# An S4 convolution with a gated FFN, forward and backward: the SSM kernel factored over 128 centred inner and 16 outer positions instead of 64 and 32

## The chip, the core and the metric

The program runs on one core of one Trainium2 chip. Its engines work side by side and each takes its instructions in order from its own queue: TensorE (matmuls, with weight loads that overlap them), VectorE, ScalarE, GpSimd, and SyncE, which here only issues DMAs. The metric is the time on the device, in microseconds (us). The kernel before took 2039.39 us, the median of five runs that lay between 2024.03 and 2045.57.

## The reference, cut to what matters

One layer with a sequence of L = 2048 positions, D = 576 channels, N = 128 states per channel and F = 4608 hidden units, in bf16. The program returns the layer's output and the gradients by twelve inputs.

```python
xn = _layernorm(x)
dt = exp(log_dt)                                   # one per channel
P  = exp((dt * (A_re + 1j*A_im))[:, :, None] * l)  # D x N x L, l = 0 .. L-1
K  = einsum("dn,dnl,dn->dl", C, P, dt * B).real    # the convolution kernel, D x L
s  = causal_convolution(xn, K) + xn * Dskip        # by FFT in the reference
g  = silu((silu(xn @ w1) * (xn @ w3)) @ w2)
out = x + s * g
# and the vector-Jacobian product of out with grad_out, by x, A_re, A_im,
# B_re, B_im, C_re, C_im, log_dt, Dskip, w1, w3, w2
```

For the gradients by A, B, C and log_dt four sums over l are needed for every channel and state: the kernel's gradient gK, and l times gK, each against the real and the imaginary part of P.

## The kernel before, in words

**Order of work.** All code is written for a planner that compiles it: `at(us)` (L83) gives the instructions that follow a due time, and the planner sorts each engine's queue by these times and by what is ready. Pools of SBUF and PSUM buffers (`tile_pool`, `bufs=n`) add waits: a tile is not written before the last reader of the buffer's former tile is done, and a pool's space is not used before the pool that held it is closed. Once built, each queue is fixed and in order.

**The factored exponential.** P at position l = AV-index and BV-index, l = BV*a + b, is the product of an outer and an inner exponential. With BV = 64 and AV = 32 (L36) the tables hold, for 16 channels (a "chunk", 36 of them), 16 x 64 inner columns called q and 16 x 32 outer ones called p or pz, 128 states deep. `build_selectors` (L336) makes two matrices of small numbers on VectorE and GpSimd: SELR and SEL. A matmul of the channels' rates with SELR gives the arguments of the real exponentials, one with SEL gives those of the phases.

**Prologue (0 to 135 us).** Layernorm, the DFT matrices dC, dSf, dSi, the selectors; then `early_exps` (L376) makes the tables E of all chunks, two chunks to a tile: matmuls into PSUM tiles of 1024 columns, Exp on ScalarE (L392), a store to E_dram. `early_spectra` (L395) makes the input's spectra beside it. The FFN's PSUM pools take the space of these two.

**Forward FFN (135 to 532 us).** `ffn_hidden` (L688): nine blocks of 512 hidden units, products of xn with w1 and w3 (L719 to L721), Silu, stores of h, of the gate and of the up product. Between its matmuls `ssm_kernel` (L418) runs, one chunk every 8.7 us by the due times. `kgen_chunk` (L455) makes the phases in PSUM tiles `et_ps` of a pool with one buffer, sine and cosine (`trig`, L326), the products q and pz with E, and v, the outer factor times B and C; q goes to Q_dram, pz to PZ_dram. `kgen_sum` (L490) contracts q with v over the 128 states, for each channel in two halves of 64 rows (L500), and copies the kernel K to the SBUF tensor KT.

**Forward tail (540 to 790 us).** `forward_tail`: h times w2 (`po`, L784), the convolution through DFTs of 1024 points in blocks of 512 (`spectra_quarter`, `conv_quarter`), a quarter of the channels at a time, and the output.

**Backward (790 to 2029 us).** `backward` (L1066) lays three things beside each other:
- 18 FFN groups of 256 hidden units (`phase6_group`, L1158, until 1627 us): the gradient of h (`ph`, L1173, copied by ScalarE at L1176), of w2 (L1201) and of w1 and w3 (L1220). The transposed gradients of gate and up go to GG_dram and GU_dram.
- Kernel gradients, 860 to 1310 us: `ssm_bwd_conv` and `conv_bwd_quarter` (L867). Inverse DFTs (`idft_tile`, matmul at L582) give gK for 128 positions at a time. ScalarE writes it from PSUM to `gk_st`, four times for each tile: two halves of the channels, plain (L927) and times l (L928). Stores bring it to gK_dram.
- Parameter sums from 1316 us on: `param_quarter` (L951). For each chunk SyncE loads the gradients into one of three buffers `gz`, whose other halves were set to zero once, transposes Q_dram to qT (L1124, called for qT), and loads pz. TensorE multiplies qT with gz (L971), VectorE multiplies with pz (L978) and sums (L980) into S_all. Their chunks have due times TC = 15 us apart.

What is left of the parameter sums runs beside the last stage, `phase6_inputs` (L1235), 1639 to 1988 us: 16 tiles of 128 positions, each with transposed loads ggc and guc (SyncE), 144 matmuls with the weights (`px`, L1263), and the layernorm's gradient (`ln_bwd_tile`, VectorE, ending at L1292 with the output tile). `phase5_final` (L983) turns S_all into the parameter gradients: four transposes on TensorE per 128 channels, then small VectorE steps.

Of the kernel before, what the change touches and what calls it, by code (L numbers as in the profile page):

```python
# [11 lines left out]
ALU = mybir.AluOpType  # L12
# [4 lines left out]
P = 128  # L17
# [5 lines left out]
class Cfg:  # L23
# [12 lines left out]
    AV: int = 32  # L36
    BV: int = 64

    @staticmethod
    def make(L, D, N, F, LS=None):  # L40
# [13 lines left out]
        assert L % 64 == 0  # L54
        c.AV = L // 64
        c.BV = 64
        assert c.AV % 2 == 0 and c.AV <= 64
# [3 lines left out]
class K:  # L61
# [24 lines left out]
    def setup_consts(self):  # L86
# [18 lines left out]
        nc.vector.tensor_copy(out=self.pcol[:], in_=icol[:])  # L105
        W = 512
# [219 lines left out]
    def trig(self, sb, m, nbits, n_el, tagp):  # L326
        nc = self.nc
        S = sb.tile([P, n_el], BF16, name="S_" + tagp)
        nc.scalar.activation(out=S[:], in_=m[:], func=ACT.Sin, scale=6.283184 / 2 ** nbits)
        A = m[:].bitcast(FP32)  # L330
        nc.scalar.activation(out=A, in_=m[:], func=ACT.Abs, scale=2.0 ** -nbits)
        C = sb.tile([P, n_el], BF16, name="C_" + tagp)
        nc.scalar.activation(out=C[:], in_=A, func=ACT.Sin, scale=-6.283184, bias=self.halfpi_col[:])
        return S, C

    def build_selectors(self, st, selp):  # L336
        nc, cfg = self.nc, self.cfg
        AV, BV, DC = cfg.AV, cfg.BV, 16
        QW, PW = DC * BV, DC * AV
        self.SEL = selp.tile([P, QW + PW], BF16, name="SEL")  # L340
        SELR = st.tile([P, QW + PW], BF16, name="SELR")
        ii = st.tile([P, QW + PW], I32, name="ii")
        i2 = st.tile([P, QW + PW], I32, name="i2")
        val = i2[:].bitcast(FP32)
        nc.gpsimd.iota(ii[:, 0:QW], pattern=[[1, DC], [0, BV]], base=0, channel_multiplier=0)
        nc.gpsimd.iota(ii[:, QW:], pattern=[[1, 2], [2, DC // 2], [0, AV]], base=0, channel_multiplier=0)
        nc.gpsimd.iota(i2[:, 0:QW], pattern=[[0, DC], [1, BV]], base=0, channel_multiplier=0)
        nc.gpsimd.iota(i2[:, QW:], pattern=[[0, DC], [1, 2], [2, AV // 2]], base=0, channel_multiplier=0)
        dl = ii[:].bitcast(FP32)
        nc.vector.tensor_copy(out=dl, in_=ii[:])  # L350
        nc.vector.tensor_copy(out=val, in_=i2[:])
        pi_ = st.tile([P, 1], I32, name="pi_")
        nc.gpsimd.iota(pi_[:], pattern=[[1, 1]], base=0, channel_multiplier=1)
        pmi = st.tile([P, 1], I32, name="pmi")
# [5 lines left out]
        rc = st.tile([P, 1], FP32, name="rc")  # L360
        nc.vector.tensor_scalar(out=rq[:], in0=self.pcol[:], scalar1=48.0, scalar2=None, op0=ALU.is_lt)
# [3 lines left out]
        nc.vector.tensor_scalar(out=rc[:], in0=self.pcol[:], scalar1=112.0, scalar2=96.0, op0=ALU.is_equal,  # L365
                                op1=ALU.mult)
        nc.vector.scalar_tensor_tensor(out=val, in0=dl, scalar=pm[:, 0:1], in1=val, op0=ALU.is_equal,
                                       op1=ALU.mult)
        nc.vector.tensor_copy(out=SELR[:, 0:QW], in_=val[:, 0:QW])
        nc.vector.tensor_scalar(out=SELR[:, QW:], in0=val[:, QW:], scalar1=float(BV), scalar2=None, op0=ALU.mult)  # L370
        for (sl, rr) in ((slice(0, QW), rq), (slice(QW, QW + PW), rp)):
            nc.gpsimd.tensor_scalar(out=self.SEL[:, sl], in0=val[:, sl], scalar1=rr[:, 0:1], scalar2=rc[:, 0:1],
                                    op0=ALU.mult, op1=ALU.add)
        return SELR

    def early_exps(self, SELR, LR_, ep, ps):  # L376
# [6 lines left out]
        for c2 in range(0, NCH, 2):  # L383
            E = ep.tile([P, 2, TW], BF16, name="E_k")
            Ef = E[:].rearrange("p c t -> p (c t)")
            for o in range(0, 2 * TW, 1024):
                pe = ps.tile([P, 1024], FP32, name="e_ps")
                for k in range(2):
                    ch, o1 = divmod(o + 512 * k, TW)
                    nc.tensor.matmul(pe[:, 512 * k:512 * k + 512], lhsT=LR_[:, c2 + ch, :], rhs=SELR[:, o1:o1 + 512],  # L390
                                     start=True, stop=True)
# [997 lines left out]
```

## Time and profile before

| | |
|---|---|
| median of five runs | 2039.39 us |
| the profiled execution, its time on the device | 2030.45 us |
| its span in the trace | 2028.7 us |
| mean granted clock of TensorE | 0.957 of full speed |
| busy: TensorE, its weight loads | 1749.6 us (86%), 1289.4 us (64%) |
| busy: VectorE, ScalarE, GpSimd | 1428.9 us (70%), 991.8 us (49%), 256.0 us (13%) |
| DMA traffic | 416.04 MB, mean 205 GB/s |
| FFN matmuls L719, 1088 of them | 273.4 us, 380 ns each |
| pr_q products L978, 288 of them on VectorE | 186.7 us, 682 ns each |
| S_all sums L980, 144 of them on VectorE | 174.1 us, 1212 ns each |
| last-stage matmuls L1263, 2304 of them | 482.5 us, 289 ns each |

All rows but the first two are of one execution, recorded by the profiler. Busy times of engines overlap, so they do not add up to the span; matmuls are pipelined, so what one costs is read from the starts of a row of them rather than from its duration. Lines such as L978 are lines of the kernel's code above. "Idle before, releaser" in a row is the time that the engine stood before these instructions and what let it go on. A share of busy time is a mean over stages with different limits; the stretches and the waits tell them apart.

### The profile page before, as it was taken

To read this page: it belongs to the slowest core of one execution; us is meant where nothing else is said; L and a number is where in the kernel's file an instruction comes from. 1 tells how busy PE (TensorE), PEld (TensorE's weight loads), DVE (VectorE), ACT (ScalarE), POOL (GpSimd) and SP (SyncE) were. 2 spreads that over 40 slices of the span, in tenths; PEclk is the share of its full clock that TensorE was granted. 3 is DMA by queue.
4 is the path that set the end of the run, shared out by engine and by line. 5 is a ranking of instruction groups with operands and counts; after the bars stand their busy time and mean duration, and the time that the engine had idled before them with its cause. 6 is when DMAs were issued, how large, how long until landed. Compare 5 with 4: busy or idle time off the path is not lost. (4 is left out here: it accounts for less than half of the span.)

```text
span 2028.7 us, 41789 instructions
## 1 busy us (share of the span) xinstructions
PE 1749.6 (86%) x17103; PEld 1289.4 (64%) x17174; DVE 1428.9 (70%) x2772; ACT 991.8 (49%) x1668; POOL 256.0 (13%) x324
## 2 busy tenths in 40 slices
PE   2789999999699996889889899889898938899991
PEld 1444444444478875778778777778776826777781
DVE  7548888888387732586884868767888555677777
ACT  2778888888545543775656746544454300000000
POOL 4003333333331102000000000100000000000000
PEclk9899999999899998899999999999999969999996
DMA  3588888897956558565473655799789599999971
GB/s 85 193 296 308 301 296 304 280 324 269 284 159 168 155 129 236 152 178 166 148 196 115 186 158 156 197 261 253 191 224 192 145 210 222 209 225 229 234 151 20
DMA packets 615088, 416.04 MB, mean 205 GB/s; under 512 B 403185, under 2 KB 560753, under 8 KB 610289
## 3 DMA queue, kind: packets, MB, share of 16 engines
q1 hardware_dynamic: 553264, 282.87, 55.5%
q0 software_dynamic: 23056, 105.00, 15.0%
q10 hardware_dynamic: 38576, 25.50, 4.6%
q8 instruction: 134, 2.20, 0.4%
q14 instruction: 58, 0.47, 0.1%
HBM read 133.01 MB, written 188.01 MB: 158 GB/s over the span
## 5 line engine op out<-in xcount | busy, mean ns | idle before, releaser
L719 PE MATMUL pgu<-wmB_w,xnT 128*128 128x512 bf16 x1088 | 273.4, 380 | 6.4 <-issue 3.2
L978 DVE TENSOR_TENSOR pr_q<-et_ps,pz 128x512 f32<-128x512 f32 x288 | 186.7, 682 | 111.1 <-PE et_ps L971 80.9
L1263 PE MATMUL px<-wTB_w,guc 128*128 128x288 bf16 x1152 | 240.5, 289 | 26.4 <-DMA guc<-GU_dram 14.2
L1263 PE MATMUL px<-wTB_w,ggc 128*128 128x288 bf16 x1152 | 242.0, 289 | 14.3 <-DMA wTB_w<-in_B_w_dram 9.4
L1220 PEld LDWEIGHTS <-xn_bf 128*128 128x128 bf16 x2304 | 226.2, 98 | 42.3 <-issue 13.9
L1173 PE MATMUL ph<-w2T,goT 128*128 128x256 bf16 x1440 | 191.7, 282 | 28.6 <-ACT gh L1176 25.9
L719 PEld LDWEIGHTS <-xnT 128*128 128x128 bf16 x1152 | 103.1, 98 | 124.0 <-issue 18.9
L980 DVE TENSOR_REDUCE S_all<-pr_q 128x16 f32<-128x1024 f32 x144 | 174.1, 1212 | 0.4
L1280 ACT ACTIVATE t<-gx 128x576 f32<-128x576 f32 x16 | 10.9, 684 | 332.9 <-DVE gx L1266 332.9
L1173 PEld LDWEIGHTS <-goT 128*128 128x128 bf16 x1440 | 141.5, 101 | 50.6 <-issue 26.7
L1201 PE MATMUL pgw<-go_o,h_n 128*128 128x288 bf16 x1152 | 156.8, 290 | 7.8 <-DVE h_n L1155 7.8
L1222 ACT CAST gw<-pgw 128x256 bf16<-128x256 f32 x144 | 54.0, 378 | 202.7 <-PE pgw L1220 195.4
L784 PE MATMUL po<-w2g,hc 128*128 128x288 bf16 x1152 | 148.6, 286 | 1.7 <-DMA hc<-H_dram 1.7
L1263 PEld LDWEIGHTS <-guc 128*128 128x128 bf16 x1152 | 113.0, 99 | 57.1 <-DMA guc<-GU_dram 15.9
L1263 PEld LDWEIGHTS <-ggc 128*128 128x128 bf16 x1152 | 112.4, 99 | 42.5 <-issue 9.5
L1220 PE MATMUL pgw<-gu_n,xn_bf 128*128 128x256 bf16 x1152 | 132.3, 272 | 5.4 <-ACT gw L1205 2.0
L1201 PEld LDWEIGHTS <-h_n 128*128 128x128 bf16 x1152 | 112.4, 99 | 37.6 <-DVE h_n L1155 8.3
L1220 PE MATMUL pgw<-gg_n,xn_bf 128*128 128x256 bf16 x1152 | 131.7, 276 | 4.4 <-ACT gw L1222 4.4
L784 PEld LDWEIGHTS <-hc 128*128 128x128 bf16 x1152 | 111.3, 98 | 29.2 <-DMA hc<-H_dram 2.2
L722 ACT ACTIVATE s_t<-pgu 128x512 bf16<-128x512 f32 x144 | 87.3, 609 | 53.7 <-PE pgu L721 53.4
L1176 ACT CAST gh<-ph 128x512 bf16<-128x512 f32 x144 | 83.7, 617 | 51.1 <-PE ph L1173 28.9
L1179 DVE TENSOR_TENSOR gu_n<-gh,gu_n 128x1024 bf16<-128x1024 bf16 x72 | 49.5, 687 | 77.6 <-ACT gh L1176 77.5
(301 smaller groups left out, 3635.3 us busy)
## 6 DMA issues: line engine op xcount, KB each, us to landing
GI_dram<-gu_t POOLq DMA_DIRECT2D x72, 512.0 KB, 5.6
H_dram<-h_t SPq DMA_DIRECT2D x72, 256.0 KB, 5.1
Q_dram<-q_k SPq DMA_DIRECT2D x36, 512.0 KB, 4.7
gg_n<-GI_dram POOLq DMA_DIRECT2D x18, 1024.0 KB, 6.1
h_n<-GI_dram POOLq DMA_DIRECT2D x18, 1024.0 KB, 8.8
GU_dram<-gu_n SPq DMA_DIRECT2D x36, 512.0 KB, 4.6
GG_dram<-gg_n SPq DMA_DIRECT2D x36, 512.0 KB, 6.7
E_dram<-E_k SPq DMA_DIRECT2D x18, 768.0 KB, 3.7
```

The lines of the kernel that those rows point to most:

```text
L719: nc.tensor.matmul(pgu[:, j], lhsT=xnT[:, c, ts], rhs=wm[w][:, c, :], start=(c == 0), stop=False)
L722: nc.scalar.activation(out=s_t[:, :, q, :], in_=pgu[:, 0].rearrange("p (g f) -> p g f", g=ng), func=ACT.Silu)
L784: nc.tensor.matmul(pos[k][:, pi_, 0:pw], lhsT=hcs[k][:, fi, :], rhs=w2[fi][:, po:po + pw], start=(fi == 0), stop=(fi == FT - 1))
L978: nc.vector.tensor_tensor(out=pr[:, r], in0=T[r][:], in1=pz[:, s + r, h * 8:h * 8 + 8, :][:, :, None, :] .to_broadcast([P, 8, 2, AV]), op= ...
L980: nc.vector.tensor_reduce(out=S_all[:, 2 * s:2 * s + 2, d0:d0 + 8].rearrange("p k d -> p d k"), in_=pr[:].rearrange("p r d k a -> p d k r ...
L1173: nc.tensor.matmul(ph[j][:, k, :].rearrange("p (a f) -> p a f", f=P), lhsT=lw, rhs=rh, start=(n == 0), stop=(n == nfull))
L1176: nc.scalar.copy(out=gh[:, j], in_=ph[j][:])
L1179: nc.vector.tensor_tensor(out=t_[:, sl], in0=gh[:].rearrange("p j t f -> p (j t) f"), in1=t_[:, sl], op=ALU.mult)
L1201: nc.tensor.matmul(pgw[pi_][:, 0:pw], lhsT=hn[:, tt, fl * P:(fl + 1) * P], rhs=go_o[:, tt, po:po + pw], start=(tt == 0), stop=(tt == LT - 1))
L1220: nc.tensor.matmul(pw_[:, 0:FG], lhsT=self.xn_bf[:, tt, c * P:(c + 1) * P], rhs=nat[:, tt, :], start=(tt == 0), stop=(tt == LT - 1))
L1222: nc.scalar.copy(out=gw[:, c, :], in_=pw_[:, 0:FG])
L1263: nc.tensor.matmul(px[pi_][:, 0:pw], lhsT=act[:, fi, :], rhs=wT[part][ai][:, f, po:po + pw], start=(fi == 0 and ai == 0), stop=(fi == FT - ...
```

## The change

The inner positions become 128 (BV) and the outer ones 16 (AV). Inner positions are counted from the middle, 63.5, and the upper half is held in reverse order. So the sine of the upper half is that of the lower with its sign turned, the cosine is the same, and phases are made for 64 of the 128 inner positions. E has 16 x (128 + 16) columns a chunk, the phases 16 x (64 + 16).

Because the rows of K now come with the upper half reversed, `flip_quarter` turns them with matmuls by a permutation, in place, once for each quarter of the channels. In the backward pass the inverse DFT uses reversed copies `imats` of its matrices, made on GpSimd, so that gK comes in the same order.

`kgen_sum` uses 128 columns of q as weights and no halves. In `conv_bwd_quarter` two positions' tiles share one PSUM tile; ScalarE writes the plain half of `gk_st`, VectorE the half that is multiplied by l; one store for a quarter replaces two. `param_quarter` takes 128 rows of gK without zeros, three chunks to a load; the qT tile has twice the columns (32 blocks of 128), its pool two buffers instead of three; products and sums are half as many. In `backward`'s call TC goes from 15 to 12 us. The selectors are made as products of small factors. The pool `kg_m` has two buffers instead of three.

```diff
-    AV: int = 32
-    BV: int = 64
+    AV: int = 16
+    BV: int = 128
...
+        nc.gpsimd.tensor_copy(out=self.flip_bf[:, 0:64], in_=self.ident_bf[:, 0:64])
+        nc.gpsimd.tensor_copy(out=self.flip_bf[:, 64:P], in_=self.ident_bf[:, 64:P][:, ::-1])
...
+        nc.vector.tensor_scalar(out=S[:, 0:n_q], in0=S[:, n_q:2 * n_q], scalar1=-1.0, scalar2=None, op0=ALU.mult)
...
-        nc.vector.scalar_tensor_tensor(out=val, in0=dl, scalar=pm[:, 0:1], in1=val, op0=ALU.is_equal,
-                                       op1=ALU.mult)
...
-        for (sl, rr) in ((slice(0, QW), rq), (slice(QW, QW + PW), rp)):
-            nc.gpsimd.tensor_scalar(out=self.SEL[:, sl], in0=val[:, sl], scalar1=rr[:, 0:1], scalar2=rc[:, 0:1],
-                                    op0=ALU.mult, op1=ALU.add)
...
+            eng.tensor_tensor(out=dst.rearrange("p (d b) -> p d b", b=w), in0=v[:, None, :].to_broadcast([P, DC, w]),
+                              in1=M[:, mi, :, None].to_broadcast([P, DC, w]), op=ALU.mult)
...
-                for k in range(2):
-                    ch, o1 = divmod(o + 512 * k, TW)
-                    nc.tensor.matmul(pe[:, 512 * k:512 * k + 512], lhsT=LR_[:, c2 + ch, :], rhs=SELR[:, o1:o1 + 512],
+                w = min(1024, 2 * TW - o)
+                cuts = sorted({o, o + w} | {b for b in (TW, o + 512) if o < b < o + w})
+                for a, b in zip(cuts, cuts[1:]):
+                    ch, o1 = divmod(a, TW)
+                    nc.tensor.matmul(pe[:, a - o:b - o], lhsT=LR_[:, c2 + ch, :], rhs=SELR[:, o1:o1 + b - a],
                                      start=True, stop=True)
-                nc.scalar.activation(out=Ef[:, o:o + 1024], in_=pe[:], func=ACT.Exp)
+                nc.scalar.activation(out=Ef[:, o:o + w], in_=pe[:, 0:w], func=ACT.Exp)
...
+                    if (ch - 2) % 9 == 8:
+                        self.flip_quarter((ch - 2) // 9, ps, T0 + TK * (ch + 1), TK)
...
+    def flip_quarter(self, g, ps, T, TK):
+        nc, LT = self.nc, self.cfg.LT
+        W = self.cfg.D // 4
+        for n, t in enumerate(range(0, LT, 3)):
+            self.at(T + TK * n / 6)
+            w = min(3, LT - t)
+            pt = ps.tile([P, 512], FP32, name="et_ps")
+            pv = pt[:, 0:w * W].rearrange("p (t d) -> p t d", t=w)
+            kt = self.KT[:, t:t + w, g * W:(g + 1) * W]
+            nc.tensor.matmul(pv, lhsT=self.flip_bf[:], rhs=kt, start=True, stop=True)
+            nc.scalar.copy(out=kt, in_=pv)
...
-            for hf in range(2):
-                for k in range(2):
-                    nc.tensor.matmul(kps[64 * hf:64 * hf + 64, dl, :], lhsT=q[:, dl, k, :],
-                                     rhs=v[:, k, e, hf * AH:(hf + 1) * AH], start=(k == 0), stop=(k == 1))
+            for k in range(2):
+                nc.tensor.matmul(kps[:, dl, :], lhsT=q[:, dl, k, :], rhs=v[:, k, e, :], start=(k == 0), stop=(k == 1))
...
+            for i, mat in enumerate((self.dC, self.dSi)):
+                im = kp.tile([P, cfg.KT, cfg.LS], BF16, name=f"imat{i}")
+                vi, vo = (t_[:].rearrange("p k (n s j) -> p (k n) s j", s=2, j=64) for t_ in (mat, im))
+                nc.gpsimd.tensor_copy(out=vo[:, :, 0], in_=vi[:, :, 0])
+                nc.gpsimd.tensor_copy(out=vo[:, :, 1], in_=vi[:, :, 1, ::-1])
+                self.imats.append(im)
...
-                for h in range(2):
-                    pv = pt[:, h * W // 2:(h + 1) * W // 2].rearrange("p (c d) -> p c d", d=8)
-                    nc.scalar.activation(out=st[:, :, 0, :, h, t], in_=pv, func=ACT.Copy, scale=1.0 / 512)
-                    nc.scalar.activation(out=st[:, :, 1, :, h, t], in_=pv, func=ACT.Copy, scale=self.lcol[:, t:t + 1])
...
+                for j in range(2):
+                    self.idft_tile(pt[:, j * W:(j + 1) * W], ZZ, oc + j, mats=self.imats)
+                pv = pt[:, 0:2 * W].rearrange("p (t d) -> p d t", t=2)
+                nc.scalar.activation(out=st[:, 0, :, t:t + 2], in_=pv, func=ACT.Copy, scale=1.0 / 512)
+                nc.vector.tensor_tensor(out=st[:, 1, :, t:t + 2], in0=pv,
+                                        in1=self.lcol[:, None, t:t + 2].to_broadcast([P, W, 2]), op=ALU.mult)
...
-            gK = gz[ch % 3]
-            for k in range(2):
-                nc.sync.dma_start(out=gK[64 * k:64 * k + 64, 1 - k].rearrange("p k f d t -> p (k f d t)"),
-                                  in_=self.gK_dram[g, :, cc].rearrange("p k f d -> p (k f d)"))
-            qT = tqp.tile([P, 16, N], BF16, name="qT")
-            self.nat_transpose(qT[:], self.Q_dram[ch])
+            if cc % GC == 0:
+                gk = gkp.tile([P, 2, 2, 8 * GC, LT], BF16, name="gk_l")
+                nc.sync.dma_start(out=gk[:].rearrange("p k h d t -> p (k h) (d t)"),
+                                  in_=self.gK_dram[g, :, :, :, 8 * cc:8 * (cc + GC), :].rearrange("p k h d t -> p (k h) (d t)"))
+            qT = tqp.tile([P, 16, 2, N], BF16, name="qT")
+            self.nat_transpose(qT[:].rearrange("p d k n -> p (d k) n"), self.Q_dram[ch])
...
-                        nc.tensor.matmul(T[r][:, dd].rearrange("p k (f t) -> p (k f) t", f=2), lhsT=qT[:, dl, :],
-                                         rhs=gK[:, r, :, :, dl, :].rearrange("p k f t -> p (k f) t"),
-                                         start=True, stop=True)
+                        nc.tensor.matmul(T[:, r, :, dd * AV:(dd + 1) * AV], lhsT=qT[:, 2 * dd + h, 1 - r, :],
+                                         rhs=gk[:, :, h, 8 * (cc % GC) + dd, :], start=True, stop=True)
...
-                    pr = qp.tile([P, 2, 8, 2, AV], FP32, name="pr_q")
-                    for r in range(2):
-                        nc.vector.tensor_tensor(out=pr[:, r], in0=T[r][:], in1=pz[:, s + r, h * 8:h * 8 + 8, :][:, :, None, :]
-                                                .to_broadcast([P, 8, 2, AV]), op=ALU.mult)
-                    nc.vector.tensor_reduce(out=S_all[:, 2 * s:2 * s + 2, d0:d0 + 8].rearrange("p k d -> p d k"),
-                                            in_=pr[:].rearrange("p r d k a -> p d k r a"), op=ALU.add, axis=AX.XY)
+                    nc.vector.tensor_tensor(out=pr[:, s].rearrange("p k r x -> p r k x"), in0=T[:],
+                                            in1=pz[:, s:s + 2, h * 8:h * 8 + 8, :].rearrange("p r d a -> p r (d a)")[
+                                                :, :, None, :].to_broadcast([P, 2, 2, 8 * AV]), op=ALU.mult)
+                nc.vector.tensor_reduce(out=S_all[:, :, d0:d0 + 8],
+                                        in_=pr[:].rearrange("p s k r (d a) -> p (s k) d r a", a=AV), op=ALU.add,
+                                        axis=AX.XY)
...
-        k.backward(560, 36, 90, 15, 18, gctx, mats)
+        k.backward(560, 36, 90, 12, 18, gctx, mats)
```

## The prediction

> **What bounds the kernel now.** I read the busy time by stretches first, then what TensorE waited for in each stage, then the order in time at the places that the change touches, and last the chain that ended the run.
>
> The stretches (columns: stretch, its length, then busy time and instructions of TensorE, of its weight loads, VectorE, ScalarE, GpSimd, then granted clock, DMA share and GB/s):
>
> ```profile
> 50.00:100.00 50.00, 37.90 (x239) 24.31 (x242) 26.51 (x43) 38.22 (x36) 0.99 (x2) 0.86 0.55 184
> 200.00:250.00 50.00, 48.74 (x472) 21.91 (x481) 42.26 (x81) 42.42 (x50) 16.73 (x16) 1.00 0.88 307
> 1000.00:1100.00 100.00, 90.80 (x920) 79.01 (x920) 58.15 (x124) 57.23 (x127) 4.29 (x8) 0.97 0.57 165
> 1400.00:1500.00 100.00, 88.94 (x934) 75.19 (x933) 82.64 (x118) 49.44 (x82) 4.83 (x9) 1.00 0.82 220
> 1700.00:1800.00 100.00, 90.94 (x867) 72.16 (x865) 65.25 (x102) 3.88 (x10) 0.00 (x0) 0.98 1.13 213
> 1900.00:2029.00 129.00, 87.80 (x787) 70.16 (x784) 90.74 (x325) 6.81 (x15) 0.00 (x0) 0.86 0.61 117
> ```
>
> TensorE is nearly full in the FFN stage (200 to 250) and 89 to 91% busy in the backward stages, so VectorE time is worth something only where TensorE waits for it. What TensorE waited for from 860 to 1310 us (kernel gradients) and, second fence, from 1310 to 1627 (parameter sums beside the FFN groups), in us, times, longest:
>
> ```profile
> PE et_ps L582 <- ACT gk_st L928: 16.5, 21, 2.1
> PE ph L1173 <- ACT gh L1176: 7.9, 6, 1.9
> ```
> ```profile
> PE ph L1173 <- ACT gh L1176: 18.1, 7, 7.7
> PE et_ps L971 <- DVE pr_q L978: 3.1, 2, 1.8
> ```
>
> SyncE's queue in the last stage has no gap: a tile's two transposes, then a chunk of the parameter sums, until 1927 us.
>
> ```profile
> 1849.61 2.88 SPq L1124 DMA_TRANSPOSE qT<-Q_dram  x1
> 1852.59 0.53 SPq L965 DMA_DIRECT2D pz<-PZ_dram  x1
> 1853.22 7.28 SPq L1124 DMA_TRANSPOSE ggc<-GG_dram  x1
> 1860.59 6.48 SPq L1124 DMA_TRANSPOSE guc<-GU_dram  x1
> ```
>
> The chain that ended last is VectorE's from 1967 us: the final parameter gradients stand between the last tile's TensorE work (ended 1988.1) and its output.
>
> ```profile
> 1953.86 10.59 DMA guc<-GU_dram
> 2013.43 0.82 DVE o L1292
> ```
>
> **The change, stage by stage.** The profiled execution took 2030.45 us (span 2028.7), 9 us below the median of the five, 2039.39. I sum against the first and carry the difference to the median.
>
> Prologue. A chunk's exponential table grows from 1536 to 2304 columns. Rows that cost it (ScalarE and TensorE in order of time):
>
> ```profile
> 129.35 5.60 ACT L392 ACTIVATE E_k<-e_ps 128x1024 bf16<-128x1024 f32 x6 [0.83 <-DMA E_dram<-E_k]
> ```
> ```profile
> 505.25 1.19 PE L500 MATMUL kps<-v_k,q_k 128*64 128x16 bf16 x64
> 506.37 1.90 PE L719 MATMUL pgu<-wmB_w,xnT 128*128 128x512 bf16 x7
> ```
>
> Six take 5.60 us: 0.93 each. A pair of chunks was 3 of them, 2.8 us; it becomes 4 and a half-sized one, 4.25 us. In the changed order 70 of the 180 table matmuls (7 pairs) follow the last spectrum matmul. The FFN can't start before them, since its PSUM is theirs. The tail was 122.6 to 134.2 us, 11.6; it becomes 7 x 4.25 plus about 0.5 a pair of waiting for the larger store (0.83 stood there), 33 us: +21. The 11 pairs that run beside the spectra add about 1. The selectors lose five wide VectorE passes (4.8 us) and 3.3 us of index generation on GpSimd, and gain two products on each; the products of B and C behind them on GpSimd, and so the layernorm behind those on ScalarE, come earlier: -3 (-5 to 0). Sum +19 (12 to 27).
>
> FFN stage. 2304 kernel-sum matmuls become 1152 with weights of 128 columns instead of 64. The 64 above start 1.12 us before the next instruction: 17.5 ns each, 40 us in all. For 128-column weights the nearest row is L971, where 24 took from 1590.44 to 1591.15, 29.6 ns: 33 us, -7. The Trainium skill speaks against any gain here ("TensorE: Matmul & The Clock Gate", LDWEIGHTS): a load costs its columns over 1.2, so half as many loads of twice the columns cost the same, and 128 columns would take 107 ns, 123 us in all, +83. Both rows above are far quicker than that, so I take the row, with 0 as the upper end. The phase matmuls shrink from 1536 to 1280 columns: 36 x 0.5 x 0.215 = -4. The flip adds 24 matmuls of 432 columns, +4, each evicted by ScalarE in about 0.54 us (between L1205's 0.41 for 288 and L1176's 0.62 for 512), through the single PSUM buffer that the phases share. In the changed order they stand 2 or 3 FFN matmuls (0.43 to 0.65 us) apart; what is queued behind a waiting flip on TensorE is the FFN itself. 24 x 0.25 = +6 (0 to 15). ScalarE loses a sixth of its three sine passes (-0.76 us a chunk) and gains 0.36 of flips; VectorE's products double for q and halve for the rest, by 0.69 and 0.42 us a row about even. Both fit beside TensorE. Sum -1 (-13 to +20; the upper end is the third rival's).
>
> Kernel gradients. 256 ScalarE evictions of 72 elements become 32 on ScalarE and 32 on VectorE of 288. The old ones show 0.80 us but start 0.32 apart, so they occupy 82 us, 1.28 a tile. They write single 2-byte elements 64 bytes apart: 4.4 ns each. The new ones write pairs 32 bytes apart. The Trainium skill ("SBUF — State Buffer", Door 1, the cachelines note) has two hits on a 16-byte line running at full rate: then 288 elements cost 0.41 us as in L1205. By the old row, 144 lines at 4.4 ns are 0.63 us, 288 elements 1.27. I take 0.7 on both engines; no row shows VectorE writing so, 0.45 (L1266) to 1.3. ScalarE is then no limit, and the 24 us of the first fence of waits mostly go; VectorE gains 22 us (14 to 42) in a chain that TensorE waits for too. -18 (-27 to +8). GpSimd's four half-reversed copies of the matrices hide, it is 4% busy; the later loads wait for nothing of them.
>
> Parameter sums. A chunk's VectorE work goes from 8 x 0.68 + 4 x 1.21 = 10.3 us to half, 5.15: 186 us in all. Only the waits in the second fence of waits can come back, and 3 of TensorE's 34 us of matmuls by halved columns. Against that the qT transpose doubles to 32 column blocks of 128; the nearest row is ggc with 36 (5.4 to 7.9 us on the queue, median landing 10.0; guc 8.3): 6.2 us and 8.5 to land, instead of 3.35 and 6.3. And its buffers fall from three to two. In the changed order, three chunks to an FFN group, every third chunk's matmuls stand about 5.3 us behind the last use of the buffer that its transpose needs. TensorE waits there 3.2 us, six times: +19. Queued behind that transpose on SyncE are pz, the kernel gradients and the next group's stores and w2T, a group early; VectorE's products for pz wait too. Relief of 10 of the 21 us of waits, and 3 of matmuls: sum +6 (-10 to +30).
>
> Last stage. The first tile's two transposes come one longer qT later: +1. Chunks now end with tile 8 instead of 14. Eight tiles took 1690.5 to 1853.9 us, 163. They now carry 11 chunks at 6.9 us of SyncE (6.2, pz 0.53, a third of gk), 9.5 a tile, beside 10.6 to 12.7 for ggc and guc: about 21.3 a tile, 170. The last seven took 134; free of chunks they are 144 x 0.1226 us and 0.15, 17.8 each, 125. Sum -3 to -4; I take -4 (-12 to +20). The final gradients run beside tiles 9 to 12 instead of after the last. From its last matmul the last tile needs its own five VectorE steps (4.5 us) and its store (about 5) and the closing 1.7: 11 instead of 40.6, -30 (-34 to -25).
>
> 19 - 1 - 18 + 6 + 1 - 4 - 30 = -27: 2003 on the profiled basis, 2012 against the median.
>
> **Rivals.** (a) Slower: the doubled transposes become the bound. For it: SyncE's queue is gapless, DMA share is 1.13 there, two buffers. Against: it has gaps before 1627 us. Each third chunk then costs 6 us more behind stores and pz, +36 instead of +6, and eight tiles 24 us each, +25 instead of -4: +32, 2071. It decides from 0.8 us of TensorE wait a chunk above my sum (27 over 33 chunks). (b) VectorE is what holds the groups: with 83% busy and a relief of 5 us a chunk, 7.5 groups shrink from 40 to 36.5 us, -26 instead of +6, and the gradients give all 27: -68, 1971. Against: the waits name VectorE for 3 us only. (c) The gain goes in the forward pass: q's store doubles, the net is 0.5 MB more a chunk, 307 GB/s at a share of 0.88 becomes about 345, which is share 1.0 at that ratio. Stores then hold back h_t and gu_t, and TensorE: +20 instead of -1, -6, 2033.
>
> **How the numbers follow.** My sum 0.45, within 1997 to 2027 of its own; (a) 0.2, (b) 0.2, (c) 0.15. A measurement of this kernel can tell about 1%, 20 us, from no change. Below 2019 lie (b) and 0.7 of my case: 0.52; above 2060 (a): 0.21; between them 0.27. The range 1971 to 2062 leaves out half of (b) and of (a).
>
> **What would show it.** The first FFN matmul near 154 us instead of 135; the FFN stage still about 395 us long; no wait for gk_st; waits of et_ps for the transposed q between 1310 and 1630; after tile 8 tiles of 17.8 us; about 11 us behind the last matmul. It is wrong if SyncE's transposes of q take over 8 us, if the new evictions take over 1.3, or if flips stop TensorE for over a microsecond each.

## The result: no faster, with large parts moved both ways

Over 43 runs the changed kernel took 2046.98 us (median, 2035.31 to 2074.09); the kernel before took 2045.41 in the 80 runs that there are of it by now. The ratio is 1.0018, 95% interval 1.0005 to 1.0032. Forecast were 2012 us against 2039, a ratio of 0.987. The profiled execution has a span of 2042.7 us, against 2028.7 before, whose execution lies 15 us below the median of its kernel; so the stages below add up to 14 us more where the medians differ by 2.

| stage, by the starts of TensorE's matmuls | before | after | difference | predicted |
|---|---|---|---|---|
| to the first FFN matmul | 135.0 | 162.4 | +27.4 | +19 |
| FFN, to the first product with w2 | 412.3 | 397.2 | -15.1 | -1 |
| forward tail, to the first group's L1201 (after: L1245) | 270.1 | 269.1 | -1.0 | 0 |
| kernel gradients, to the eleventh group | 494.5 | 466.4 | -28.1 | -18 |
| parameter sums, to the first tile | 327.3 | 363.9 | +36.6 | +6 and +1 |
| first eight tiles | 196.0 | 206.7 | +10.7 | +7 |
| last eight tiles | 153.0 | 169.8 | +16.8 | -11 |
| behind the last matmul | 40.6 | 7.0 | -33.6 | -30 |

The prediction's -4 for the last stage was +7 and -11. The same stretches of the profile as before (columns as there):

```profile
200.00:250.00 50.00, 48.79 (x371) 21.13 (x376) 45.08 (x89) 42.33 (x53) 21.27 (x17) 1.00 1.01 366
1000.00:1100.00 100.00, 90.84 (x962) 79.37 (x960) 66.13 (x140) 49.85 (x101) 4.30 (x8) 1.00 0.61 186
1400.00:1500.00 100.00, 85.14 (x898) 72.00 (x896) 57.97 (x84) 47.64 (x75) 4.29 (x8) 0.91 1.01 223
1700.00:1800.00 100.00, 84.05 (x794) 65.64 (x793) 42.02 (x68) 3.10 (x8) 0.00 (x0) 0.91 1.13 226
```

Between 1400 and 1500 us VectorE fell from 82.6 to 58.0 us, and TensorE, which was to gain by that, fell from 88.9 to 85.1; the DMA share rose from 0.82 to 1.01. In the FFN stage the DMA engines moved 366 GB/s instead of 307 and TensorE lost nothing.

What TensorE waited for, in us, times, longest; first from 860 to 1310 us, then from 1310 to 1659:

```profile
PE et_ps L623 <- DVE gx L991: 5.7, 4, 1.6
...
PE et_ps L623 <- DVE gk_st L971: 4.3, 2, 2.1
```
```profile
PE et_ps L1015 <- DMA qT<-Q_dram: 51.5, 8, 8.8
PE ph L1217 <- ACT gh L1220: 8.4, 1, 8.4
PE et_ps L1015 <- DVE pr_q L1020: 0.6, 1, 0.6
```

The 16.5 us for ScalarE's gk_st are gone, and 4.3 for VectorE's came. In the second stretch the two rows that were shown before, 18.1 for ScalarE and 3.1 for VectorE, became 8.4 and 0.6, and 51.5 for the transposed q came. The granted clock of TensorE was lower there too, 0.89 against 0.96, and its busy time rose from 286.3 to 294.8 us. How much of that the waits themselves brought about, no run separates. In order of time one of them looks like this, on TensorE and then on SyncE:

```profile
1429.29 0.56 PE L1015 MATMUL et_ps<-gk_l,qT 128*128 128x32 bf16 x16
1429.70 3.65 PE L1217 MATMUL ph<-w2T,goT 128*128 128x256 bf16 x32
1441.85 0.32 PE L1015 MATMUL et_ps<-gk_l,qT 128*128 128x32 bf16 x5 [8.50 <-DMA qT<-Q_dram]
```
```profile
1428.31 6.04 SPq L1168 DMA_TRANSPOSE qT<-Q_dram  x1
1434.45 0.53 SPq L1010 DMA_DIRECT2D pz<-PZ_dram  x1
1435.07 13.99 SPq L1168 DMA_TRANSPOSE qT<-Q_dram  x2
```

A chunk's matmuls release its buffer at 1428, the transpose of two chunks later is issued then, and its data is there 13.5 us later, 8.5 after TensorE has run out of other work. In the chain that ended last, seven such landings stand between 1347 and 1612 us, 7.4 to 13.5 us long.

SyncE in the last tiles, and the end of the chain:

```profile
1926.41 0.54 SPq L1104 DMA_DIRECT2D out_dram<-gl_bf  x1
1927.00 0.51 SPq L1106 DMA_DIRECT2D out_dram<-gl_bf  x1
1943.46 0.47 SPq L80 DMA_DIRECT2D out_dram<-gout  x1
1944.02 6.62 SPq L1168 DMA_TRANSPOSE ggc<-GG_dram  x1
1950.73 9.29 SPq L1168 DMA_TRANSPOSE guc<-GU_dram  x1
```
```profile
1963.89 71.66 PE px L1307 x573
...
2038.89 0.82 DVE o L1336
```

One store of a final gradient stands from 1927.5 to 1943.5 in front of a tile's two transposes, waiting for VectorE. After it four tiles run freely, 71.66 us, and the last tile's steps end 4.2 us after its last matmul.

### The profile page after: what moved, and what is told of

Its sections match the earlier page's. It is cut to its first block, busy times and chain, and to the rows that moved or that the text cites. A ratio compares the mean times of both kernels' runs of the same rounds, so it can differ in the third digit from the quotient of the medians.

```text
span 2042.7 us, 39175 instructions
## 1 busy us (share of the span) xinstructions
PE 1754.1 (86%) x16061; PEld 1282.0 (63%) x16118; DVE 1280.3 (63%) x2632; ACT 941.8 (46%) x1504; POOL 260.1 (13%) x329
## 4 chain that ended last, share of the span: by engine, by line
PE 32%; DVE 19%; DMA 10%; SPq 7%; ACT 2%; issue 2%; ACTq 0%; DVEq 0%; POOLq 0%
PE px L1307 8%; PE pgw L1264 7%; SPq L1168 6%; DMA qT<-Q_dram 5%; PE po L825 5%; PE pgw L1245 4%; DVE cm_t L648 3%; PE ph L1217 3%; DVE cm_t L645 2%; DVE Z L646 2%; PE et_ps L667 2%; DVE Z L651 1%; DVE Z L650 1%; DMA gg_n<-GI_dram 1%; DMA guc<-GU_dram 1%
## 5 line engine op out<-in xcount | busy, mean ns | idle before, releaser
L760 PE MATMUL pgu<-wmB_w,xnT 128*128 128x512 bf16 x1104 | 278.9, 379 | 4.0 <-ACT gu_t L765 1.5
L1307 PE MATMUL px<-wTB_w,ggc 128*128 128x288 bf16 x1152 | 246.3, 294 | 29.4 <-DMA ggc<-GG_dram 15.1
L1307 PE MATMUL px<-wTB_w,guc 128*128 128x288 bf16 x1152 | 245.6, 294 | 28.9 <-DMA guc<-GU_dram 17.4
L1020 DVE TENSOR_TENSOR pr_q<-et_ps,pz 128x512 f32<-128x512 f32 x144 | 94.3, 683 | 184.7 <-PE et_ps L1015 126.7
L1217 PE MATMUL ph<-w2T,goT 128*128 128x256 bf16 x1440 | 185.9, 279 | 10.7 <-ACT gh L1220 10.1
L1245 PE MATMUL pgw<-go_o,h_n 128*128 128x288 bf16 x1152 | 165.7, 301 | 9.0 <-DVE h_n L1199 9.0
L1245 PEld LDWEIGHTS <-h_n 128*128 128x128 bf16 x1152 | 116.6, 102 | 42.4 <-DVE h_n L1199 9.6
L1310 DVE TENSOR_TENSOR gx<-px,gxs 128x288 f32<-128x288 f32 x32 | 13.3, 451 | 182.6 <-PE px L1307 182.6
L1015 PE MATMUL et_ps<-gk_l,qT 128*128 128x32 bf16 x1152 | 51.9, 181 | 68.0 <-DMA qT<-Q_dram 63.0
```

The source lines that it names most:

```text
L760: nc.tensor.matmul(pgu[:, j], lhsT=xnT[:, c, ts], rhs=wm[w][:, c, :], start=(c == 0), stop=False)
L1020: nc.vector.tensor_tensor(out=pr[:, s].rearrange("p k r x -> p r k x"), in0=T[:], in1=pz[:, s:s + 2, h * 8:h * 8 + 8, :].rearrange("p r d ...
L1217: nc.tensor.matmul(ph[j][:, k, :].rearrange("p (a f) -> p a f", f=P), lhsT=lw, rhs=rh, start=(n == 0), stop=(n == nfull))
L1245: nc.tensor.matmul(pgw[pi_][:, 0:pw], lhsT=hn[:, tt, fl * P:(fl + 1) * P], rhs=go_o[:, tt, po:po + pw], start=(tt == 0), stop=(tt == LT - 1))
L1307: nc.tensor.matmul(px[pi_][:, 0:pw], lhsT=act[:, fi, :], rhs=wT[part][ai][:, f, po:po + pw], start=(fi == 0 and ai == 0), stop=(fi == FT - ...
```

## The experiments

Ratios are to the kernel before, run on the same chip, with 95% intervals. Stage lengths are of one profiled execution each, and single ones scatter: in kernels that are alike there the parameter sums differ by up to 16 us, the first eight tiles by up to 8 and every other stage by up to 4.

**Three buffers for the transposed q.**

```diff
-self.tc.tile_pool(name="g_k", bufs=3, side="right")
+self.tc.tile_pool(name="g_k", bufs=2, side="right")
...
-self.tc.tile_pool(name="g_t", bufs=2, side="right")
+self.tc.tile_pool(name="g_t", bufs=3, side="right")
...
+self.tc.tile_pool(name="g_p", bufs=1, side="right") as self.prp
...
-pr = qp.tile([P, 2, 2, 2, 8 * AV], FP32, name="pr_q")
+pr = self.prp.tile([P, 2, 2, 2, 8 * AV], FP32, name="pr_q")
```

> The changed kernel with three buffers for the transposed q instead of two (the space comes from the loads of gK, two buffers instead of three, and from one buffer for the products pr_q, which only VectorE uses). The order of TensorE's work is that of the changed kernel. Theory A, the wait is the chain 'buffer released, transpose issued, 10 us to land' with two buffers: TensorE's waits for the transposed q between the eleventh group and the first tile of the last stage (51.5 us in 8) fall below 15 us, that stage goes from 364 to about 325 us, and the whole time by about 40 us. Theory B, the doubled transposes load the DMA engines and TensorE waits for data whatever the buffers: the waits stay above 40 us and the stage above 355 us.

Measured: 0.9953 (0.9917 to 0.9989); parameter sums 361.9 us against 363.9. The waits for q fell as theory A said, and the stage did not. TensorE's waits from 1296 to 1657 us:

```profile
PE ph L1218 <- ACT gh L1221: 18.6, 7, 8.1
PE pgw L1265 <- DVE gu_n L1224: 11.1, 7, 1.9
PE et_ps L1016 <- DMA qT<-Q_dram: 10.2, 4, 4.6
PE pgw L1265 <- ACT gw L1267: 8.7, 3, 5.0
```

ScalarE in its turn waits for SyncE's traffic, 25.9 us in 4 for the stores of the up gradients (gu_n) alone. One of the four in order of time, on SyncE and then on ScalarE:

```profile
1415.51 5.37 SPq L1169 DMA_TRANSPOSE qT<-Q_dram  x1
1420.97 0.54 SPq L1231 DMA_DIRECT2D GU_dram<-gu_n  x1
```
```profile
1421.36 0.70 ACT L1250 CAST gw<-pgw 128x288 bf16<-128x288 f32 x2 [0.22 <-PE pgw L1246]
1425.63 0.35 ACTq L1251 DMA_DIRECT2D out_dram<-gw  x1
1426.08 0.37 ACT L1267 CAST gw<-pgw 128x256 bf16<-128x256 f32 x1 [4.01 <-DMA GU_dram<-gu_n]
```

SyncE issues its store only when the transpose of q before it is issued. ScalarE's own store of a weight gradient (L1251) waits for a semaphore on which SyncE's store counts its landing, at 1425.56, and in ScalarE's queue everything else waits behind L1251. In the same way L1251 is held seven times in this stage, 2.0 to 7.9 us each: four times by such a store, once by a load of pz, twice by a transpose of q.

So neither A nor B as they were stated: the chain of two buffers was removed, and another limit stood just behind it.

**Final stores on GpSimd's queue**, alone and with the three buffers. All stores of `phase5_final` are changed like this one:

```diff
-                    self.dma(aps[oname][do:do + dsz, :], ob[v])
+                    self.dma(aps[oname][do:do + dsz, :], ob[v], eng=nc.gpsimd)
```

> The changed kernel with the stores of the final parameter gradients issued by GpSimd's queue, which is empty in the last stage, instead of SyncE and ScalarE. Theory C, the stores stand in front of the tiles' transposes on SyncE and hold them while they wait for VectorE's results: the last eight tiles, 169.9 us in the changed kernel, take 142 to 148, and the whole time falls by 22 to 28 us. Theory D, VectorE's 200 small steps of the final gradients or the extra transposes of q hold the tiles: the last eight stay above 162 us.

> Both together, three buffers for the transposed q and the final stores on GpSimd's queue. If A and C hold and do not overlap, the time falls by 60 to 70 us from the changed kernel's, to about 0.97 of the kernel before. If the losses are one and the same shortage of DMA time, it falls by less than 30.

Measured: 0.9939 (0.9909 to 0.9970) alone, 0.9877 (0.9830 to 0.9924) together. From the changed kernel's 1.0018 these are -0.8% and -1.4%, 16 and 29 us: less than C alone and A with C had promised. The 29 us lie within what was expected if the losses were one shortage of DMA time (less than 30); the waits below speak for something else in the last tiles. In the run of both the last eight tiles took 160.8 us instead of 169.8, between the two expectations, and the waits there, from 1848 us on, say why:

```profile
PE px L1308 <- DVE gx L1311: 14.2, 4, 13.0
```

With the stores out of the way VectorE itself holds a tile: it does the final gradients in one row before it reads the tile's PSUM.

**Chunks due every 15 us again.**

```diff
-        k.backward(560, 36, 90, 12, 18, gctx, mats)
+        k.backward(560, 36, 90, 15, 18, gctx, mats)
```

> The changed kernel with the chunks of the parameter sums due every 15 us again instead of 12. TensorE's order then has 2 to 3 chunks in a group instead of 3, and 15 instead of 10 chunks are left when the last stage starts; the final gradients move behind the fifteenth tile. Theory A (two buffers, latency): fewer chunks in a row, so the groups' stage gains 15 to 25 us (to about 345), and the last stage gives back as much or more: whole time within 15 us of the changed kernel. Theory of the schedule, that 12 us is what costs: more than 25 us faster than the changed kernel.

Measured: 0.9918 (0.9870 to 0.9966), 20 us below the changed kernel by the ratios. That lies between the two expectations, 15 and 25 us. Its profiled execution took 2005.99 us, far below its median of 2030.81, so its stages are read for direction only: parameter sums 323.6, first eight tiles 191.1, last eight 157.6, and 34.7 behind the last matmul. Fewer chunks before the last stage help there, and the tail comes back.

**Final gradients spread.** Due 18 us apart for the five pieces, six result buffers, on top of three buffers and GpSimd's stores.

```diff
+            t5 = self.tc.cur_priority
             for c, (do, dsz) in enumerate(cfg.dch):
+                self.tc.cur_priority = t5 + 18000 * c
```

> Three buffers for the transposed q and the final stores on GpSimd's queue as in the run of both, and the five pieces of the final gradients due one a tile (18 us apart) instead of all at once, with six buffers for their results instead of three. VectorE's order then has some 47 small steps between two tiles' own. Theory D, what was left of the loss in the last eight tiles (160.8 us there, 142 if free) is VectorE doing the final gradients in one row before the tiles' own steps: the last eight take 143 to 148 and the time falls by another 12 to 18 us. Rival, the transposes' own DMA time or the clock holds the tiles: the last eight stay above 155.

Measured: 0.9849 (0.9768 to 0.9930); last eight tiles 151.3 us instead of 160.8. No wait for gx is left there; the one wait in all of it is

```profile
PE px L1310 <- DMA guc<-GU_dram: 4.6, 2, 4.3
```

Theory D holds for 9.5 us (the spreading and the six result buffers were not tried apart), and with C's 9.0 the two explain 18.5 of the 28 us between 169.8 and the predicted 142.

**Half of each q transposed.**

```diff
-            self.nat_transpose(qT[:].rearrange("p d k n -> p (d k) n"), self.Q_dram[ch])
+            self.nat_transpose(qT[:, 0:8].rearrange("p d k n -> p (d k) n"), self.Q_dram[ch, :, 0:2048])
...
-lhsT=qT[:, 2 * dd + h, 1 - r, :]
+lhsT=qT[:, (2 * dd + h) % 8, 1 - r, :]
```

> The changed kernel with only half of each q transposed (16 blocks of columns instead of 32; each half is used twice, so half of the work on the parameter sums is left out as data, not as instructions on TensorE and VectorE). TensorE's order and the number of chunks in a group are unchanged. Theory B, the groups' stage is long because the doubled transposes use up the DMA engines: it falls from 364 to 330 to 340 us, and the share of busy DMA there from 0.96 to below 0.88. Theory S, it is long because 25 chunks instead of 20 come before the last stage: it stays above 355.

Measured: 0.9873 (0.9807 to 0.9938); DMA share 0.77 from 1312 to 1640 us, parameter sums 350.7 us, and TensorE still waits 50.7 us for q in 9. The stage lies between the two expectations. With two buffers the chain of release, issue and landing holds TensorE even at half the traffic.

**Evictions unpaired.**

```diff
-                nc.scalar.activation(out=st[:, 0, :, t:t + 2], in_=pv, func=ACT.Copy, scale=1.0 / 512)
-                nc.vector.tensor_tensor(out=st[:, 1, :, t:t + 2], in0=pv, in1=self.lcol[:, None, t:t + 2].to_broadcast([P, W, 2]), op=ALU.mult)
+                for j in range(2):
+                    nc.scalar.activation(out=st[:, 0, :, t + j], in_=pv[:, :, j], func=ACT.Copy, scale=1.0 / 512)
+                    nc.vector.tensor_scalar(out=st[:, 1, :, t + j], in0=pv[:, :, j], scalar1=self.lcol[:, t + j:t + j + 1], scalar2=None, op0=ALU.mult)
```

> The changed kernel with each pair's eviction undone: twice as many evictions of gK, 144 elements each, single 2-byte elements 32 bytes apart. If pairing is what the gain in the kernel gradients comes from (pairs at full rate, 0.44 us for 288 elements): an eviction of 144 takes about 0.63 us as the old ones would by their rate, and the stage from the first group to the eleventh goes from 466 to 480 or more. If it comes from fewer evictions and from VectorE taking half: evictions take about 0.3 us and the stage stays below 471.

Measured: 1.0185 (1.0107 to 1.0263); kernel gradients 504.2 us against 466.4. The tile gk_st (min, median, max in ns), changed kernel first, then this run:

```profile
L970 ACT ACTIVATE gk_st<-et_ps x32: 422/438/448, 872.5 to 1254.6; 128x288 bf16<-128x288 f32 x32
L971 DVE TENSOR_TENSOR gk_st<-et_ps,lcol x32: 451/452/458, 873.0 to 1255.8; 128x288 bf16<-128x288 f32 x32
```
```profile
L971 ACT ACTIVATE gk_st<-et_ps x64: 768/800/1127, 871.8 to 1296.8; 128x144 bf16<-128x144 f32 x64
L972 DVE TENSOR_SCALAR gk_st<-et_ps,lcol x64: 803/836/1030, 872.6 to 1297.6; 128x144 bf16<-128x144 f32 x64
```

Half the elements take nearly twice as long from start to end when they are single. That length counts here because the program lets an eviction begin only after the other engine's on the same PSUM tile: in the unpaired run ScalarE stood idle 23.8 us, 24 times, until VectorE's was done. Where two of ScalarE's follow each other without such a wait, the second starts 0.31 us after the first (18 cases), as in the kernel before (0.32). Unpaired, the stage is 10 us longer than there (494.5), so the split between two engines loses without pairs. What pairs would gain without the split was not tried.

**The kernel before with 12 us.**

```diff
-        k.backward(560, 36, 90, 15, 18, gctx, mats)
+        k.backward(560, 36, 90, 12, 18, gctx, mats)
```

> The kernel before with the chunks due every 12 us instead of 15, the one part of the change that is a number in the schedule. 25 chunks instead of 19 then stand before the last stage and the final gradients beside tiles 9 to 12. Theory B: with the old transposes this does little harm, the groups' stage goes from 327 to at most 345 (VectorE's 10.3 us for each of 6 chunks more, partly hidden). Theory S: it goes to 355 or more. In both, the 34 us saved behind the last tile are given back for the most part by the last tiles (theories C and D): their last eight take 165 or more instead of 153, and the whole time is within 15 us of the kernel before.

Measured: 1.0084 (1.0051 to 1.0117). Parameter sums 357.9 us, first eight tiles 213.1, last eight 178.2, tail 7.0. Theory S's number came, though not by transposes: from 1311 to 1669 us TensorE waits 2.1 us for q, 38 for ScalarE and 9.7 for VectorE. From 1655 us on the largest wait is for VectorE, whose work on a chunk is 10.3 us there, with 19.6 for loads of weights and 17.8 for guc close behind:

```profile
PE et_ps L971 <- DVE pr_q L978: 20.2, 5, 7.5
```

So 12 us do not pay without the rest of the change; that they need its relief of VectorE is likely by this row and not tested. The 34 us behind the last tile are given back here too, as expected.

**Half transposes and three buffers.** The edits of the two runs above, and no others:

```diff
+self.tc.tile_pool(name="g_t", bufs=3, side="right")
...
+            self.nat_transpose(qT[:, 0:8].rearrange("p d k n -> p (d k) n"), self.Q_dram[ch, :, 0:2048])
```

> Half of each q transposed and three buffers for it (half of the parameter sums' data is left out; the other work and the number of chunks in a group are unchanged). Each of the two alone left the groups' stage at 351 to 362 us. If two limits stand close together, the buffers' chain and the doubled transposes on SyncE's queue and the DMA engines, taking both away gives 325 to 335. If the number of chunks before the last stage is the limit (theory S), it stays at 348 or more.

Measured: 0.9712 (0.9647 to 0.9778). Parameter sums 316.5 us, first eight tiles 182.2: 47 and 24 us less than in the changed kernel, where three buffers alone gave 2 to 13 us (361.9, 351.1 and 354.0 in three kernels) and half transposes 13. ScalarE's waits of 25.9 us for the stores of gu_n are gone, and so is the wait for q. The waits that the profile names for TensorE in this stage fall from 58 us with three buffers alone to 30, and its busy time from 297.7 to 285.5 us, at a granted clock of 0.96 against 0.93: 40 of the 45 us between the two.

Two limits, then, of nearly the same height, and 25 chunks before the last stage cost nothing once both are gone. Half transposes take less of SyncE's queue and of the DMA engines at once, so this run does not tell which of the two is the second limit. Theory S falls. The last eight tiles, which this run doesn't touch, stay at 168.7.

**Chunks every 13.5 and 14 us**, with three buffers, GpSimd's stores and the final gradients spread 14 us apart.

```diff
-        k.backward(560, 36, 90, 12, 18, gctx, mats)
+        k.backward(560, 36, 90, 13.5, 18, gctx, mats)
```

> Three buffers, final stores on GpSimd's queue, final gradients spread over tiles 11 to 14, and chunks due every 13.5 us: 22 or 23 of them before the last stage. From the runs so far (12 us: 354 us for the groups, 199 and 151 for the last stage's halves, 7 behind it; 15 us: 324, 191, 158, 35): groups 335 to 345, first eight tiles 193 to 197, last eight 148 to 156, tail 7 to 10. Time 0.975 to 0.985 of the kernel before.

> As the run with 13.5 us, with chunks due every 14 us: the final gradients then stand beside tiles 12 to 15. Groups 330 to 342, first eight tiles 191 to 196, last eight 150 to 158, tail 7 to 18 as the last piece of the gradients ends with the last tile. Time 0.973 to 0.985 of the kernel before.

Measured: 0.9881 (0.9848 to 0.9914) and 0.9932 (0.9898 to 0.9967). Parameter sums 341.6 and 339.9 us as expected, first eight tiles 205.4 and 200.2 and not 191 to 197, tail 12.6 and 29.8, both longer than expected, and neither total reached the 0.985 that was to be its upper end. Fewer chunks before the last stage are more beside its tiles. These two, the run of both edits and the spread one all beat both kernels, by 0.7 to 1.5% of the kernel before; all four intervals overlap, so which is best stays open.

**Every second exponential left to VectorE as a copy.**

```diff
-                nc.scalar.activation(out=Ef[:, o:o + w], in_=pe[:, 0:w], func=ACT.Exp)
+                if o // 1024 % 2 == 0:
+                    nc.scalar.activation(out=Ef[:, o:o + w], in_=pe[:, 0:w], func=ACT.Exp)
+                else:
+                    nc.vector.tensor_copy(out=Ef[:, o:o + w], in_=pe[:, 0:w])
```

> The changed kernel with every second exponential of the tables E replaced by a plain copy on VectorE (the exponential of half of the table's columns is left out; matmuls and stores are unchanged). Theory P, ScalarE's 4.37 us of exponentials for each pair of chunks pace the prologue's tail: a pair takes 3.5 us or less there and the first FFN matmul comes at 135 to 148 us instead of 162. Rival, TensorE's matmuls at the lower clock or the larger stores pace it: pairs stay near 5 us and the first FFN matmul at 156 or later.

Measured: the first FFN matmul at 157.1 us. ScalarE in the tail of the prologue, changed kernel first (a pair of chunks is these two lines), then this run:

```profile
131.56 1.94 ACT L416 ACTIVATE E_k<-e_ps 128x1024 bf16<-128x1024 f32 x2 [0.66 <-PE e_ps L414]
133.68 2.43 ACT L416 ACTIVATE E_k<-e_ps 128x1024 bf16<-128x1024 f32 x3 [0.18 <-PE e_ps L414]
```
```profile
139.69 1.02 ACT L417 ACTIVATE E_k<-e_ps 128x1024 bf16<-128x1024 f32 x1 [0.94 <-PE e_ps L414]
141.81 1.02 ACT L417 ACTIVATE E_k<-e_ps 128x1024 bf16<-128x1024 f32 x1 [1.10 <-PE e_ps L414]
143.30 0.60 ACT L417 ACTIVATE E_k<-e_ps 128x512 bf16<-128x512 f32 x1 [0.47 <-PE e_ps L414]
```

ScalarE's share of a pair fell from 4.37 to 2.64 us, and a pair from 5.2 to 4.3 to 4.7: ScalarE now waits for TensorE, 12.1 us in 18. Theory P's 5.3 us are small, the more so as other runs with this prologue reach that matmul between 159.3 and 162.9 us, and the rival's range was met; that it is TensorE and not the stores is read from the releaser, not tested alone. The rival had named a lower clock, and the windows of the tail, before and after the change, show it (0.68 in the column after the busy times):

```profile
122.00:135.00 13.00, 6.93 (x26) 2.34 (x25) 0.76 (x1) 11.40 (x13) 0.00 (x0) 1.00 0.81 301
125.00:162.00 37.00, 26.66 (x73) 8.88 (x74) 1.28 (x2) 31.39 (x37) 0.00 (x0) 0.68 0.73 264
```

In this run it was 0.89 from 125 to 157 us, so ScalarE's share and the clock changed together and are not separated.

**Transposes of q on ScalarE's queue**, the last ten and then all, on top of the spread run.

```diff
-        self.nc.sync.dma_start_transpose(out=dst, in_=src)
+        (eng or self.nc.sync).dma_start_transpose(out=dst, in_=src)
...
+                               nc.scalar if ch >= 26 else None)
```

> The run with three buffers, final stores on GpSimd's queue and spread final gradients, with the last ten transposes of q issued by ScalarE instead of SyncE (ScalarE is nearly idle in the last stage). Theory Q, SyncE's one queue is what the doubled transposes fill (5.3 us of issuing each beside 10.6 for a tile's two): the first eight tiles fall from 199 to 183 to 190 us, near the 182 seen with half transposes. Theory E, the DMA engines themselves are full: the first eight stay at 196 or more.

> The same with all 36 transposes of q issued by ScalarE. There the groups' evictions stand behind them in ScalarE's queue, 5 to 8 us each time. Theory Q: what SyncE is relieved of shows in the groups' stage less what ScalarE's blocked evictions cost; three transposes a group are 16 us of ScalarE against its 19 us of slack in a group of 41, so the stage comes to 345 to 375 us against 354. Theory E: nothing is relieved and the evictions' delay is all that shows, 375 or more.

Measured: 1.0053 (1.0027 to 1.0079) and 1.0440 (1.0411 to 1.0469). With the last ten the first eight tiles took 231.6 us, against 199.2: neither theory's number. SyncE's waits from 1640 to 1910 us:

```profile
SPq L1172 <- DMA qT<-Q_dram: 87.3, 9, 14.3
```

SyncE's transposes wait until ScalarE's have landed. The program holds these waits: the Trainium skill ("DMA: Bandwidth & Descriptors", Silent corruption: two transposing streams in flight at once) says why, that a later stream's first transpose must wait for the full completion of the earlier stream's. On one queue a transpose is issued about 5 us after the last; across two queues the landing, 8.6 us here, stands between them. With all on ScalarE the parameter sums took 430.4 us. So SyncE's queue could not be told from the DMA engines in this way, and which of them sets the price of the doubled transposes stays open.

## Why the prediction was wrong, step by step

**Prologue, +27.4 for +19: a term mis-sized.** ScalarE was taken to set a pair's time with 0.5 us beside it; it is 5.2 us: TensorE waits for ScalarE 22 times and ScalarE for TensorE 7 times on two PSUM buffers, and TensorE's granted clock was 0.68 there, against 1.00 in the tail before. What each adds is not separated. The tail behind the spectra took 37.0 us where 33 were forecast. The 3 us from earlier selectors did not come: the first exponential starts at 63.5 us, before at 62.7.

**FFN, -15.1 for -1.** The flips were overpriced: one waited 1.0 us, and they start 0.18 us before what follows, 4 us in all instead of 10. The kernel sums save more than 7: each to the start of the next matmul they went from 54.9 to 34.8 us. Within a row a start follows by 16.5 ns before and 26.0 after, which is 8 to 10 of the 20 us; the rest are the ends of rows, as many as before (118 and 117) but 0.07 us long instead of 0.16, and why is not shown. The phase matmuls save 7 instead of 4, and the FFN's own take 7 us more, part of which are records that the trace before lacks. The third rival, stores holding TensorE at 345 GB/s, did not happen at 366. For the weights of 128 columns the row was right, and the skill's 107 ns ("TensorE: Matmul & The Clock Gate", LDWEIGHTS) were no price per matmul: the recorded loads last 95 to 99 ns, near the rule, but overlap, and the starts follow by 26 ns.

**Kernel gradients, -28.1 for -18: a term mis-sized.** The evictions take 0.44 and 0.45 us; I took 0.7, between the old row and the Trainium skill's rule on 16-byte lines ("SBUF — State Buffer", Door 1), and the rule's 0.41 was the nearer. ScalarE's waits of 16.5 us went as forecast. The unpaired run shows that with the work on two engines the pairs decide the stage; it does not show that they alone bring the gain.

**Parameter sums, +36.6 for +7: the step that failed.** "TensorE waits there 3.2 us, six times" was 6.4 us, eight times: the landings that TensorE waited for took 7.4 to 13.5 us, not 8.5, and there were two more of them. The relief of VectorE came as forecast and is worth little. What the step did not hold is that this wait covers another: with the third buffer SyncE's stores and loads among the doubled transposes hold ScalarE's stores, and TensorE waits for ScalarE instead. The prediction had seen what is queued behind a transpose on SyncE, but not that ScalarE waits for it. Only both edits together, 316.5 us, take the loss away, at half of q's data; they also bring the clock back to 0.96.

**Last stage, +27.5 for -3: the second failure.** The first eight tiles came within 4 us as a difference, but not as a sum: they took 206.7 us where 170 were summed, against 196.0 before and not 163, since the stretch that the prediction read begins 51 us after the first tile. "The final gradients run beside tiles 9 to 12" was costed at nothing, and it costs what the tail saves: SyncE's in-order queue holds a tile's transposes behind a store that waits for VectorE (9.0 us), and VectorE's in-order queue holds the tile's PSUM behind 200 small steps (9.5 us). The kernel before with 12 us loses there too, 178.2 against 153.0. The 9 us that the last eight tiles still have above 142 were not traced further.

**Behind the last matmul, -33.6 for -30.** Right.

The first rival, doubled transposes as the bound, had +36 and +25 for the two stages that failed; they came to +36.6 and +27.5. For the second that is luck: the rival put it into the eight tiles with chunks, which lost 10.7, and had none of the 16.8 that the final gradients' tiles lost. Its total of 2071 was too high mostly because the FFN and kernel-gradient stages gave 24 us more than the sum that it shared, against 8 less from the prologue.

## What to carry to other kernels

When a transfer is made larger and its buffers fewer, price its landing by the longest that stand in the trace at that place, and ask what stands behind it in its queue and who waits for that; two limits of the same height hide each other, so take away both before concluding that neither matters. Work moved from behind the end to beside the last stage is free only if every queue it is put on, the stores' as well as the engine's, has nothing of that stage standing behind it: spread it. Where another engine waits for the end of a PSUM eviction that writes strided 2-byte elements, write pairs.

## What the runs showed of the hardware that was not expected

An eviction that writes 144 single 2-byte elements, 32 bytes apart, lasts 0.80 us on ScalarE and 0.84 on VectorE from start to end; 288 elements in pairs last 0.44 and 0.45. ScalarE starts a next single one after 0.31 us, so the length is paid only where something waits for the end. Matmuls with 128 columns of weights and 16 moving columns follow each other in 26 ns, with 64 columns in 16.5. Transposes issued from two queues took turns at the price of a landing each, 87.3 us of waiting in the run with ten of them moved. ScalarE's stores of weight gradients were held 2.0 to 7.9 us by the landing of transfers from SyncE's queue, since the program counts both on one semaphore, and ScalarE's evictions stood behind them.
